# Attention, a low-rank mix, two feed-forward layers and a Fourier mix on one core: tables, decoding, mix and Fourier step placed elsewhere

## The chip, the core and the metric

The kernel runs on one core of a Trainium2 chip. The metric is the device time of one execution in microseconds. The engines are named as in the profile: PE (TensorE, matrix products and transposes), PEld (its weight loads), DVE (VectorE), ACT (ScalarE), POOL (GpSimd) and SP (SyncE, which here only issues transfers). Each engine works through its own instructions in the order in which they stand.

## What is computed

The reference, cut to what matters (x has 2 batches of 768 tokens with 512 columns; attention has 8 heads of width 64):

```
attn: scores = q k^T / 8 - slope_h * dist   (only keys j < n_global, or 0 <= i-j < n_local)
      x      = softmax(scores) v            (heads side by side: 512 columns)
mix:  u = x + (V^T U^T x along the tokens)  (U 768x32, V 32x768)
ffn:  x = u + relu(u @ w1) @ w2             (w1 512x2048, w2 2048x512)
fft:  u = x + real(fft over tokens and columns of x)
      un = (u - mean) / sqrt(var + 1e-6)
ffn:  out = u + relu(un @ w1') @ w2'
```

## The kernel before, in words

Float32 products of full accuracy are made of three matmuls each: every operand is split in a high part (float32r) and a low part (the rest). The weights U, V, w1, w2 arrive as 64-bit doubles. `decode` (L150) turns them into float32 in four operations, on ACT L155 and then on DVE L157, L159 and L161; a decoded chunk of weights (`w_load`, L110, brings it) is written to a scratch in DRAM for the later blocks and split into `wh` (ACT L170) and `wo` (POOL L173, two halves).

The program runs in three stages.

**Attention.** `setup` (L44) loads the first q, k and v, lets POOL write distances into the buffer `vb1` (`rel_make`), and lets DVE make from them two bias tables `dist0` and `dist1` of 1024 columns (`attn_setup`, L391; the second is half the first, ACT L405); a flag `oki` decides a branch. Then `attn` (L452) goes through 24 units (a pair of heads c, a pair of token tiles j and j+3), two units per iteration d = 0 to 11, with three more iterations for the end. An iteration makes scores on PE (L472, L477) in four PSUM banks `acc`, adds the bias and takes the minimum on DVE (L494), exponentials on ACT (L506), transposes on PE (L515), copies them out on DVE (L526) or ACT (L524), multiplies by v one iteration later (L540, two PSUM banks `sd`), and turns the result back two iterations later (L553, DVE L561) into `xall`. Loads of q and k (`qk_load`, L426) and of v (`v_load`, L437) for pair c+2 go out when the buffers of pair c are free. SP issues them in its order.

**Beside the attention** `arm` (L854) steps other generators, one item per step of attention: `lr_setup` decodes U and V, `w_first` decodes the first two chunks of weights, `lr(0)` makes the low-rank sum of batch 0 (L330, L337) and its mix (L346, DVE L347), with transposes of the mixed tiles into `uT` (PE L270, ACT L272, DVE L273) which the first feed-forward step needs. All of these take the two PSUM banks `h`, as the attention's transposes do.

**Feed-forward.** `ffn` (L177) runs 96 steps c, 16 for each of three blocks of four token tiles and each of two layers. A step is 12 matmuls L194 (into `h`), a ReLU split in two (ACT L201, DVE L202) and 12 matmuls L222 (into the four `acc` banks); it yields four times. `drive` (L828) puts side work between yields: after each of n yields a counter grows by a rate, and each whole unit takes one item of a side generator; what is left after n yields is drained at once. Beside block 1 (c = 16 to 31) transposes stand, beside block 2 (c = 32 to 47) the loads of the Fourier tables, a wait until six tiles are done (`lead`), the Fourier step of batch 0 (`fft(0)`: folds on DVE L693 to L711, matmuls L742, L746, L753, L766, L779, L792) and layernorm with transposes of tiles 0 to 3 (`norm`, L811). Layer 1 begins at c = 48 and needs those four. `fft(1)` stands beside c = 48 to 63. A scheduler sets each engine's final order from the program; instructions marked with `keep` stay in program order.

Of the kernel before, what the change touches and what calls it, by code (L numbers as in the profile page):

```python
# [7 lines left out]
F32 = mybir.dt.float32  # L8
# [29 lines left out]
class Prog:  # L38
# [5 lines left out]
    def setup(self, ctx):  # L44
# [13 lines left out]
        nf = cp.tile([P, 2, 2], F32, name="nf")  # L58
        nc.vector.tensor_copy(nf, ni)
        hi = cp.tile([P, 2], F32, name="nhi")  # L60
        nc.vector.scalar_tensor_tensor(hi, nf[:, :, 0], 0.0, nf[:, :, 1], ALU.is_lt, ALU.add)
        nv = cp.tile([P, 4], F32, name="nv")
        nc.vector.scalar_tensor_tensor(nv[:, 0:2], hi, 4294967296.0, nf[:, :, 0], ALU.mult, ALU.add)
        self.ng, self.nl, self.nl4 = nv[:, 0:1], nv[:, 1:2], nv[:, 2:3]
        self.attn_setup()
        nc.vector.tensor_scalar(ok[:, 0:1], nv[0:1, 0:1], float(NG_MAX), None, ALU.is_le)
        nc.vector.tensor_scalar(ok[:, 1:2], nv[0:1, 1:2], 1.0, None, ALU.is_ge)
        nc.vector.scalar_tensor_tensor(ok[:, 0:1], nv[0:1, 1:2], float(NL_MAX), ok[:, 0:1], ALU.is_le, ALU.mult)
        nc.vector.tensor_tensor(ok[:, 0:1], ok[:, 0:1], ok[:, 1:2], ALU.mult)
        oki = cp.tile([1, 1], I32, name="oki")  # L70
        nc.vector.tensor_copy(oki, ok[:, 0:1])
# [192 lines left out]
    def transpose_in(self, layer, i, src):  # L264
# [3 lines left out]
        tp = self.psum("tr")  # L268
# [47 lines left out]
    def w_first(self):  # L316
        for c in range(2):
            for z in range(4):
                self.w_word(c, z)
                yield  # L320
        self.w_split(0)
        yield


    def lr(self, b, pool, tiles):
# [12 lines left out]
        R = pool.tile([P, D], FR, tag="R", bufs=1, name=f"R{b}")  # L338
        nc.scalar.copy(R, rps)
        nc.vector.tensor_tensor(R[64:128, :], rps[64:128, :], R[64:128, :].bitcast(F32), ALU.subtract)  # L340
        yield
        for t in range(NT):
            i = b * NT + t
            x = self.x[i]
            hp = self.psum("m")
# [16 lines left out]
    def rel_make(self):  # L362
# [12 lines left out]

        blocks = ((0, 0, 1), (3, 128, -1), (4, 256, -1), (5, 511, -1), (1, 0, 1), (2, 128, 1), (6, 127, -1), (7, 255, -1))
# [10 lines left out]
        iota(self.key[:, 0:P], 0, 1, 0)  # L387
        iota(self.key[:, P:], 0, 1, 0)

    def attn_setup(self):  # L390
        nc = self.nc  # L391
# [50 lines left out]
    def attn(self, pool):  # L442
# [75 lines left out]
        def turned(d, g):  # L518
# [4 lines left out]
            if g == 1 or (g == 3 and d % 2 == 1):  # L523
# [41 lines left out]
        for d in range(ND2 + 3):  # L565
# [288 lines left out]
def arm(tc, pg, fast):  # L854
    with ExitStack() as ctx1:
# [186 lines left out]
```

## Time and profile before

| quantity | value |
|---|---|
| time, median of 3 runs | 701.17 us (700.15 to 703.96) |
| the profiled execution's own time | 699.38 us |
| its span from first to last instruction | 697.5 us |
| PE busy in the span | 666.3 us (96%) |
| DVE busy | 362.4 us (52%) |
| POOL busy | 311.5 us (45%) |
| ACT busy | 283.2 us (41%) |
| mean granted clock of PE | 0.989 of full |

The profiled execution took 1.88 us more than its span and 1.79 us less than the median. Busy time of an engine is a sum over stages, so it doesn't say by itself which engine ends last in a stage; that is read in the windows, the timelines and the chain of waits.

### The profile page before, as it was taken

The numbers are of one execution on the slowest core, as the hardware profiler recorded it, in microseconds if no ns is written. First come the engines' busy times: TensorE is split into PE (matmuls) and PEld (weight loads), VectorE is DVE, ScalarE is ACT, GpSimd is POOL, SyncE is SP. The second block draws the span as 40 slices with busy tenths as digits, with TensorE's granted clock in tenths as the row PEclk, the third lists the DMA queues.
The fourth block names the chain that finished last, engine by engine and source line by source line (L and its number), as shares of the span: only waits on it lengthen the run. The fifth ranks groups of instructions, "written<-read, shape, count | busy, mean of one in ns | idle before, by whom it ended". The sixth has DMA issues, their size and how long they took to land.

```text
span 697.5 us, 9519 instructions
## 1 busy us (share of the span) xinstructions
PE 666.3 (96%) x3498; PEld 546.7 (78%) x3498; DVE 362.4 (52%) x702; ACT 283.2 (41%) x513; POOL 311.5 (45%) x288
## 2 busy tenths in 40 slices
PE   7998889999999999999999879999999999999996
PEld 6877566887778888887888767888888888888885
DVE  6899677888839453388535878116632111211112
ACT  5898642543434434334433324222323333232330
POOL 4022102554675654557443637344644444544441
PEclk9999999999999999999999989999999999999999
DMA  8967503787897777666744321312142232332301
GB/s 283 326 239 268 182 1 97 220 249 248 251 363 242 250 251 246 233 215 220 268 176 146 133 85 38 114 61 90 61 151 92 93 113 95 132 110 96 115 32 66
DMA packets 34424, 115.98 MB, mean 166 GB/s; under 512 B 4096, under 2 KB 5568, under 8 KB 31296
## 3 DMA queue, kind: packets, MB, share of 16 engines
q1 hardware_dynamic: 32544, 111.04, 47.3%
q0 software_dynamic: 1392, 3.65, 1.6%
q8 instruction: 29, 0.48, 0.3%
q10 hardware_dynamic: 432, 0.59, 0.3%
q14 instruction: 27, 0.22, 0.1%
HBM read 95.34 MB, written 19.92 MB: 165 GB/s over the span
## 4 chain that ended last, share of the span: by engine, by line
PE 73%; DVE 15%; ACT 4%; DMA 3%; issue 2%; POOL 2%; SPq 0%; DVEq 0%; ACTq 0%; POOLq 0%
PE ps_acc L222 32%; PE ps_h L194 31%; DVE wr L159 2%; DVE w L161 2%; DVE p L494 2%; PE ps_sd L540 2%; POOL wo L173 2%; DMA qk<-qkg 1%; PE ps_sd L270 1%; ACT wr L155 1%; PE ps_sd L742 1%; PE ps_sd L766 1%; PE ps_acc L472 1%; DVE pt L526 1%; DVE xall L561 1%
## 5 line engine op out<-in xcount | busy, mean ns | idle before, releaser
L173 POOL TENSOR_TENSOR wo<-w,wh 128x512 fp32r<-128x512 f32 x192 | 270.2, 1428 | 271.0 <-ACT wh L170 270.8
L194 PE MATMUL ps_h<-uT,wh 128*128 128x512 f32 x768 | 238.7, 392 | 1.3 <-ACT uT L272 1.3
L202 DVE SCALAR_TENSOR_TENSOR gl<-ps_h,gh 128x512 fp32r<-128x512 f32 x96 | 66.0, 687 | 234.0 <-ACT gh L201 233.9
L170 ACT CAST wh<-w 128x1024 fp32r<-128x1024 f32 x96 | 101.0, 1052 | 196.7 <-PE ps_acc L222 122.9
L194 PEld LDWEIGHTS ps_h<-uT,wh 128*128 128x128 f32 x768 | 143.2, 188 | 32.5 <-issue 2.2
L222 PE MATMUL ps_acc<-wh,gl 128*128 128x512 f32 x384 | 151.4, 394 | 2.3 <-DVE gl L202 2.1
L222 PE MATMUL ps_acc<-wh,gh 128*128 128x512 f32 x384 | 152.1, 396 | 0.0
L194 PE MATMUL ps_h<-uT,wo 128*128 128x512 f32 x384 | 150.1, 391 | 1.9 <-POOL wo L173 1.9
L222 PE MATMUL ps_acc<-wo,gh 128*128 128x512 f32 x384 | 150.4, 392 | 0.0
L201 ACT ACTIVATE gh<-ps_h 128x512 fp32r<-128x512 f32 x96 | 57.4, 598 | 139.9 <-PE ps_h L194 137.2
L222 PEld LDWEIGHTS ps_acc<-wh,gl 128*128 128x128 f32 x384 | 72.5, 189 | 20.1 <-DVE gl L202 4.8
L194 PEld LDWEIGHTS ps_h<-uT,wo 128*128 128x128 f32 x384 | 72.1, 188 | 18.1 <-POOL wo L173 2.9
L222 PEld LDWEIGHTS ps_acc<-wo,gh 128*128 128x128 f32 x384 | 72.7, 189 | 14.1
L222 PEld LDWEIGHTS ps_acc<-wh,gh 128*128 128x128 f32 x384 | 72.6, 189 | 13.8
L159 DVE SCALAR_TENSOR_TENSOR wr<-wr 128x1024 int32<-128x1024 int32 x32 | 48.2, 1506 | 12.2 <-ACT wr L155 10.9
L506 ACT ACTIVATE p<-p,m 128x256 f32<-128x256 f32 (+2 forms) x96 | 47.6, 498 | 9.7 <-DVE m L494 9.5
L494 DVE CUSTOM_DVE_ANT_0 p<-ps_acc,dist 128x256 f32<-128x256 f32 (+2 forms) x96 | 34.9, 418 | 7.6 <-PE ps_acc L472 4.2
L155 ACT ACTIVATE wr<-wr 128x1024 f32<-128x1024 f32 x32 | 36.7, 1147 | 0.0
L472 PE MATMUL ps_acc<-qk 64*128 64x256 f32 (+1 forms) x192 | 24.6, 381 | 2.9 <-DVE m L494 2.3
L161 DVE SCALAR_TENSOR_TENSOR w<-wr 128x1024 int32<-128x1024 int32 x16 | 26.4, 1652 | 0.8
L515 PE MATMUL ps_h<-ident,p 128*128 128x128 f32 x144 | 22.1, 288 | 2.9 <-DVE xall L561 2.2
L540 PE MATMUL ps_sd<-pt,vb 128*64 128x128 f32 x384 | 23.6, 276 | 0.0
(150 smaller groups left out, 537.5 us busy)
## 6 DMA issues: line engine op xcount, KB each, us to landing
w<-wscr SPq DMA_DIRECT2D x80, 512.0 KB, 3.3
wr<-wl SPq DMA_DIRECT2D x17, 1024.0 KB, 7.5
wr<-wl SPq DMA_DIRECT2D x60, 256.0 KB, 5.5
wscr<-w SPq DMA_DIRECT2D x16, 512.0 KB, 7.7
wscr<-wd SPq DMA_DIRECT2D x16, 512.0 KB, 2.9
qk<-qkg SPq DMA_DIRECT2D x7, 1088.0 KB, 7.1
vb<-vw SPq DMA_DIRECT2D x8, 768.0 KB, 4.7
out<-qk SPq DMA_DIRECT2D x11, 256.0 KB, 3.4
```

The source lines that it names most:

```text
L155: keep(nc.scalar.activation(hi.bitcast(F32), hi.bitcast(F32), AF.Copy, scale=2.0 ** -112))
L159: nc.vector.scalar_tensor_tensor(lo, hi, 3, lo, ALU.logical_shift_left, ALU.bitwise_or)
L161: nc.vector.scalar_tensor_tensor(out.bitcast(I32), hi, -2147483648, lo, ALU.bitwise_and, ALU.bitwise_or)
L170: nc.scalar.copy(hi, raw)
L173: nc.gpsimd.tensor_tensor(lo[:, h], raw[:, h], hi[:, h].bitcast(F32), ALU.subtract)
L194: nc.tensor.matmul(hp, lhsT=w[:, s], rhs=u[:, dd, :], start=n == 0, stop=n == 11)
L201: nc.scalar.activation(gh, hp, AF.Relu)
L202: nc.vector.scalar_tensor_tensor(gl, hp, 0.0, gh.bitcast(F32), ALU.max, ALU.subtract)
L222: nc.tensor.matmul(acc[t], lhsT=g[:, s], rhs=w[:, D:2 * D], start=pf == 0 and m == 0, stop=pf == NF - 1 and m == 2)
L494: keep(nc.vector.tensor_tensor_reduce(out=T[z][:, s], in0=sp[z][:, s], in1=self.dist[z][:, dcol[t]:dcol[t] + width[t]], op0=ALU.add, op1=A ...
L506: keep(nc.scalar.activation(T[z][:, s], T[z][:, s], AF.Exp, bias=m[:, z, y:y + 1], scale=-1.0, accum_out=sm[:, u % 2, y, z:z + 1]))
L540: keep(nc.tensor.matmul(pv[z * HD:(z + 1) * HD, g:g + P], lhsT=v[:, vc, z * HD:(z + 1) * HD], rhs=pt[z][:, o:o + P], start=i == 0, stop=i ...
```

## The change

It has four parts.

1. `setup`: the integers n are used directly (the cast into `nf` goes), the flag takes three operations and not five, and `attn_setup` is split. Part 0 makes the columns that the first unit needs (0 to 128, 384 to 768) ahead of the branch, part 1 the other columns (128 to 384, 768 to 1024) after the first unit's L494. All of it stays in program order.
2. `turned`: in the last iteration (d = 11) all copies go to ACT.
3. `arm`: the items are in another order. The decoding of U comes later, that of the first weights one operation per iteration half, that of V behind it, that of the second weights behind the low-rank sum. `lr` is cut in `lr_sum` and `lr_mix`; the mix of batch 0 and its transposes take banks `acc`, at the end of attention.
4. The Fourier tables are loaded beside block 1, so that `fft(0)` and `norm` are the only side work of block 2, at a rate of 0.55.

```diff
-        nc.vector.tensor_copy(nf, ni)
-        nc.vector.scalar_tensor_tensor(hi, nf[:, :, 0], 0.0, nf[:, :, 1], ALU.is_lt, ALU.add)
+        nc.vector.scalar_tensor_tensor(hi, ni[:, :, 0], 0.0, ni[:, :, 1], ALU.is_lt, ALU.add)
...
-        self.attn_setup()
...
+        self.attn_setup(0)
...
+        iota(self.key[:, 0:P], 0, 1, 0)
+        iota(self.key[:, P:], 0, 1, 0)
         blocks = ((0, 0, 1), (3, 128, -1), (4, 256, -1), (5, 511, -1), (1, 0, 1), (2, 128, 1), (6, 127, -1), (7, 255, -1))
...
-        for c0, c1, blocks in ((0, 128, ((0, P),)), (384, 768, ((512, 32),)), (128, 384, ((256, 32),)),
-                               (768, WTAB, ((896, 32),))):
+        for c0, c1, blocks in (((0, 128, ((0, P),)), (384, 768, ((512, 32),))),
+                               ((128, 384, ((256, 32),)), (768, WTAB, ((896, 32),))))[part]:
...
-            if g == 1 or (g == 3 and d % 2 == 1):
+            if g == 1 or (g == 3 and d % 2 == 1) or d == ND2 - 1:
...
                 for y in range(2):
                     soft(u0, y)
                     exps(u0, y)
+                if d == 0:
+                    self.attn_setup(1)
                 soft(u1, 0)
...
-                for _ in pg.lr_setup(lp):
-                    step(att, 1)
+                step(att, 3)
                 pg.w_load(1)
-                step(att, 2)
+                low = pg.lr_setup(lp)
+                for _ in range(2):
+                    next(low)
+                    step(att, 2)
+                for _ in pg.w_first(0):
+                    step(att, 2)
                 pg.w_load(2)
-                for _ in pg.w_first():
+                for _ in low:
                     step(att, 1)
                 while pg.heads < 8:
                     step(att, 1)
-                for _ in pg.lr(0, lp, range(0, 4)):
+                step(att, 1)
+                for _ in chain(pg.lr_sum(0, lp), pg.w_first(1)):
                     step(att, 1)
                 while not pg.att_tail:
                     step(att, 1)
+                pg.w_split(0)
+                mix = pg.lr_mix(0, range(0, 4), "sc")
+                for _ in range(4):
+                    step(mix, 2)
+                    step(att, 1)
+                drain(mix)
...
-        drive(main, 64, pg.tr_gen(0, range(8, 12), pg.x), 0.3)
...
-        drive(main, 64, chain(pg.fft_tables(), lead(pg, 6), pg.fft(0), pg.norm(range(0, 4))), 0.5)
+        drive(main, 64, chain(pg.tr_gen(0, range(8, 12), pg.x), pg.fft_tables()), 0.3)
+        drive(main, 64, chain(lead(pg, 6), pg.fft(0), pg.norm(range(0, 4))), 0.55)
```

Where instructions come to stand, as the two built programs have them (line numbers of the changed kernel are three lower in the attention and the feed-forward part):

DVE at the start, the kernel before: the tables (`dist_66` is dist0, `vb_69` is vb1) ahead of the first unit's reads (`L494`).

```order
L71 CAST oki<-ok 1x1
L400 TENSOR_SCALAR dist_66<-vb_69,nv 128x128
L401 TENSOR_TENSOR dist_66<-dist_66,vb_69 128x128
L400 TENSOR_SCALAR dist_66<-vb_69,nv 128x384
L401 TENSOR_TENSOR dist_66<-dist_66,vb_69 128x384
L400 TENSOR_SCALAR dist_66<-vb_69,nv 128x256
L396 TENSOR_SCALAR vb_69<-vb_69,nv 128x160
L401 TENSOR_TENSOR dist_66<-dist_66,vb_69 128x256
L404 SCALAR_TENSOR_TENSOR dist_66<-vb_69,nv,dist_66 128x128
L404 SCALAR_TENSOR_TENSOR dist_66<-vb_69,nv,dist_66 128x32 x2
L400 TENSOR_SCALAR dist_66<-vb_69,nv 128x256
L401 TENSOR_TENSOR dist_66<-dist_66,vb_69 128x256
```

DVE at the same place, the changed kernel, from the last table operation ahead of the branch to the second unit.

```order
L401 SCALAR_TENSOR_TENSOR dist_66<-vb_69,nv,dist_66 128x32
L936 TENSOR_LOAD oki
L937 COMPARE_AND_BRANCH
L491 ISA p_208,m_210<-ps_acc,dist_66 128x128
L491 ISA m_210 128x1
L491 ISA p_209,m_210<-ps_acc,dist_67 128x128
L491 ISA m_210 128x1
L491 ISA p_208,m_210<-ps_acc,dist_66 128x384
L491 ISA m_210 128x1
L491 ISA p_209,m_210<-ps_acc,dist_67 128x384
L491 ISA m_210 128x1
L397 TENSOR_SCALAR dist_66<-vb_69,nv 128x256
```

The last two of the four column ranges (six operations, of which the last row shows the first) moved from ahead of the first unit to behind it.

DVE at the end of attention, the kernel before, from the copy behind the last L494 (`uT_1298` is the low part for the first feed-forward block, `xall_200` batch 0, `xall_201` batch 1).

```order
L526 COPY pt_1273<-ps_sd 128x512
L347 TENSOR_TENSOR xall_200<-ps_h,xall_200 128x512
L699 MEMSET vb_68 128x1
L273 TENSOR_TENSOR uT_1298<-ps_h,uT_1297 128x4x128
L549 TENSOR_SCALAR sm_922<-sm_922 128x8
L550 RECIPROCAL sm_922<-sm_922 128x8
L561 TENSOR_TENSOR xall_201<-ps_h,sm_922 128x2x128 x2
L526 COPY pt_1320<-ps_h 128x512
L347 TENSOR_TENSOR xall_200<-ps_h,xall_200 128x512
L526 COPY pt_1340<-ps_h 128x512
L526 COPY pt_1344<-ps_sd 128x512
L273 TENSOR_TENSOR uT_1298<-ps_h,uT_1297 128x4x128
```

The same place in the changed kernel (`uT_1385` is the low part, `xall_188` batch 0, `wr_589` the second weights).

```order
L334 TENSOR_TENSOR R_1271<-ps_h,R_1271 64x512
L546 TENSOR_SCALAR sm_904<-sm_904 128x8
L547 RECIPROCAL sm_904<-sm_904 128x8
L558 TENSOR_TENSOR xall_189<-ps_h,sm_904 128x2x128 x2
L523 COPY pt_1288<-ps_h 128x512
L154 TENSOR_SCALAR wr_589<-wr_589 128x1024
L344 TENSOR_TENSOR xall_188<-ps_acc,xall_188 128x512
L156 SCALAR_TENSOR_TENSOR wr_589<-wr_589 128x1024
L546 TENSOR_SCALAR sm_1004<-sm_1004 128x8
L344 TENSOR_TENSOR xall_188<-ps_acc,xall_188 128x512
L547 RECIPROCAL sm_1004<-sm_1004 128x8
L158 SCALAR_TENSOR_TENSOR w_1290<-wr_589 128x1024
```

The mix reads `ps_acc` where it read `ps_h`, the decoding of the second weights moved in between, and the copies of the last iteration are gone from DVE.

PE where layer 0 ends (c = 48), the kernel before: the last Fourier matmuls and the four transposes for layer 1.

```order
L779 MATMUL ps_sd<-c_2870,fpt_3302 128x258
L781 MATMUL ps_sd<-sgn,fpr_3303 128x258
L270 MATMUL ps_sd<-ident,vb_68 128x128 x4
L222 MATMUL ps_acc<-wh_3625,gh_3706 128x512
L222 MATMUL ps_acc<-wo_3626,gh_3706 128x512
L222 MATMUL ps_acc<-wh_3625,gl_3707 128x512
L270 MATMUL ps_sd<-ident,vb_68 128x128 x4
L222 MATMUL ps_acc<-wh_3625,gh_3706 128x512
```

In the changed kernel the first of these four transposes stands five steps sooner, ahead of the matmuls of a later step.

```order
L219 MATMUL ps_acc<-wh_3364,gh_3458 128x512
L219 MATMUL ps_acc<-wo_3365,gh_3458 128x512
L219 MATMUL ps_acc<-wh_3364,gl_3459 128x512
L267 MATMUL ps_sd<-ident,vb_68 128x128 x4
L191 MATMUL ps_h<-uT_2217,wh_3501 128x512
```

The four transposes stand at c = 43, 44, 45 and 46; the first Fourier matmuls (`L741`, L742 of before), which stood at c = 41, stand at c = 35 and 36, and `L745` (L746 of before), which needs `em`, at c = 36.

## Rows read from the trace of the kernel before

**Rows 1.** The page, part 1: busy time, share of the span and instructions.

```profile
PE 666.3 (96%) x3498; PEld 546.7 (78%) x3498; DVE 362.4 (52%) x702; ACT 283.2 (41%) x513; POOL 311.5 (45%) x288
```

**Rows 2.** Windows, us: length; busy (count) PE, PEld, DVE, ACT, POOL; PEclk; DMA; GB/s.

```profile
60.00:80.00 20.00, 16.66 (x157) 11.79 (x158) 15.32 (x54) 15.21 (x43) 5.85 (x5) 0.91 0.74 254
400.00:420.00 20.00, 15.27 (x60) 11.67 (x61) 14.25 (x29) 4.49 (x7) 7.33 (x12) 0.83 0.26 80
```

**Rows 3.** The chain that ended last, 0 to 130 us: start, length, what.

```profile
12.98 10.08 DMA qk<-qkg
23.24 0.84 POOL qk L430
```

**Rows 4.** Timeline of DVE at the start: start, length, operation, count, idle before.

```profile
8.55 0.34 DVE L400 TENSOR_SCALAR dist<-vb,nv 128x256 f32<-128x256 f32 x1
...
9.39 0.25 DVE L404 SCALAR_TENSOR_TENSOR dist<-vb,nv,dist 128x32 f32<-128x32 f32 x1
10.24 0.29 DVE L494 CUSTOM_DVE_ANT_0 p<-ps_acc,dist 128x128 f32<-128x128 f32 x1 [0.60 <-DVE dist L404]
...
11.62 0.42 DVE L494 CUSTOM_DVE_ANT_0 p<-ps_acc,dist 128x256 f32<-128x256 f32 x1
```

**Rows 5.** Timeline of PE in attention, same columns.

```profile
24.12 0.93 PE L472 MATMUL ps_acc<-qk 64*128 64x128 f32 x8 [0.55 <-POOL qk L430]
...
30.45 1.79 PE L472 MATMUL ps_acc<-qk 64*128 64x256 f32 x16
...
74.37 3.60 PE L330 MATMUL ps_h<-xall,ur 128*32 128x512 f32 x12 [2.42 <-DVE xall L561]
...
86.41 2.00 PE L472 MATMUL ps_acc<-qk 64*128 64x256 f32 x16
...
111.03 0.73 PE L194 MATMUL ps_h<-uT,wh 128*128 128x512 f32 x2
```

**Rows 6.** Timeline of DVE in attention, two stretches, same columns.

```profile
55.66 0.69 DVE L157 TENSOR_SCALAR wr<-wr 128x1024 int32<-128x1024 int32 x1
56.45 1.23 DVE L159 SCALAR_TENSOR_TENSOR wr<-wr 128x1024 int32<-128x1024 int32 x1
...
58.30 1.21 DVE L161 SCALAR_TENSOR_TENSOR w<-wr 128x1024 int32<-128x1024 int32 x1
...
90.61 0.42 DVE L494 CUSTOM_DVE_ANT_0 p<-ps_acc,dist 128x256 f32<-128x256 f32 x1
...
107.49 0.69 DVE L273 TENSOR_TENSOR uT<-ps_h,uT 128x512 fp32r<-128x512 f32 x1 [2.17 <-ACT uT L272]
...
108.60 0.76 DVE L561 TENSOR_TENSOR xall<-ps_h,sm 128x256 f32<-128x256 f32 x2
```

**Rows 7.** Timeline of PE, c = 36 and c = 47 to 48.

```profile
318.77 0.50 PE L194 MATMUL ps_h<-uT,wo 128*128 128x512 f32 x1 [1.49 <-POOL wo L173]
...
403.21 1.09 PE L270 MATMUL ps_sd<-ident,vb 128*128 128x128 f32 x4 [3.45 <-DVE mv L818]
...
410.74 1.23 PE L194 MATMUL ps_h<-uT,wh 128*128 128x512 f32 x3 [1.30 <-ACT uT L272]
```

**Rows 8.** One window of 1 us, columns as in rows 2.

```profile
404.00:405.00 1.00, 1.00 (x5) 0.80 (x4) 0.77 (x2) 0.59 (x1) 0.58 (x2) 0.50 0.25 98
```

**Rows 9.** Timeline of DVE in the folds of fft(0).

```profile
302.06 2.04 DVE L159 SCALAR_TENSOR_TENSOR wr<-wr 128x1024 int32<-128x1024 int32 x1
...
318.92 1.51 DVE L693 TENSOR_TENSOR qk<-dist 128x255 f32<-128x255 f32 x1
...
321.21 0.42 DVE L704 TENSOR_TENSOR em<-qk,em 1x258 fp32r<-1x258 f32 x1
```

**Rows 10.** Timeline of POOL, the split of weights.

```profile
301.72 3.52 POOL L173 TENSOR_TENSOR wo<-w,wh 128x512 fp32r<-128x512 f32 x2 [2.91 <-ACT wh L170]
```

**Rows 11.** Timeline of PE, where steps 41 and 42 begin.

```profile
347.48 0.63 PE L194 MATMUL ps_h<-uT,wh 128*128 128x512 f32 x2
...
354.76 0.63 PE L194 MATMUL ps_h<-uT,wh 128*128 128x512 f32 x2
```

More of the change, by code (lines that the diff above doesn't have):

```diff
@@ L262, in uT_tiles, with transpose_in @@
         return self.uT[key]
-    def transpose_in(self, layer, i, src):
+    def transpose_in(self, layer, i, src, kind="tr"):
         nc = self.nc
@@ L267, in transpose_in @@
         s = slice((i % 4) * P, (i % 4 + 1) * P)
-        tp = self.psum("tr")
+        tp = self.psum(kind)
         for dd in range(ND):
@@ L314, in lr_setup, with w_first, lr_sum @@
         yield
[L316 to L325, printed above, removed]
+    def w_first(self, c):
+        for z in range(4):
+            self.w_word(c, z)
+            yield
+    def lr_sum(self, b, pool):
         nc = self.nc
@@ L337, in lr @@
         nc.tensor.matmul(rps, lhsT=self.band.rearrange("p z r -> p (z r)"), rhs=part, start=True, stop=True)
-        R = pool.tile([P, D], FR, tag="R", bufs=1, name=f"R{b}")
+        self.R = R = pool.tile([P, D], FR, tag="R", bufs=1, name=f"R{b}")
         nc.scalar.copy(R, rps)
@@ L341, in lr, with lr_mix @@
         yield
+    def lr_mix(self, b, tiles, kind="m"):
+        nc, R = self.nc, self.R
         for t in range(NT):
@@ L344, in lr @@
             x = self.x[i]
-            hp = self.psum("m")
+            hp = self.psum(kind)
             nc.tensor.matmul(hp, lhsT=self.vs[:, t * P:(t + 1) * P], rhs=R, start=True, stop=True)
@@ L349, in lr @@
             if t > 0 and i - 1 in tiles:
-                self.transpose_in(0, i - 1, self.x[i - 1])
+                self.transpose_in(0, i - 1, self.x[i - 1], kind)
                 yield
         if b * NT + NT - 1 in tiles:
-            self.transpose_in(0, b * NT + NT - 1, self.x[b * NT + NT - 1])
+            self.transpose_in(0, b * NT + NT - 1, self.x[b * NT + NT - 1], kind)
             yield
@@ L386, in rel_make, with attn_setup @@
                 nc.gpsimd.memset(rel[0:1, 3 * P:5 * P], float(-4 * FAR))
[L387 to L391, printed above, removed]
+    def attn_setup(self, part):
+        nc, keep = self.nc, self.tc.keep_in_program_order
         rel, key = self.rel, self.key
@@ L891, in arm @@
                 drain(pg.lr_setup(lp))
-                drain(pg.w_first())
+                for c in range(2):
+                    drain(pg.w_first(c))
+                pg.w_split(0)
                 pg.attn_any(pool)
-                drain(pg.lr(0, lp, range(0, 4)))
+                drain(chain(pg.lr_sum(0, lp), pg.lr_mix(0, range(0, 4))))
         pg.side_mode = True
-        drive(main, 64 - ahead, chain(pg.lr(1, lp, range(6, 8)), pg.tr_gen(0, range(4, 6), pg.x)), 0.45)
-        drive(main, 64, pg.tr_gen(0, range(8, 12), pg.x), 0.3)
+        drive(main, 64 - ahead, chain(pg.lr_sum(1, lp), lambda: pg.lr_mix(1, range(6, 8)),
+                                      pg.tr_gen(0, range(4, 6), pg.x)), 0.45)
     with ExitStack() as ctx3:
         pg.fft_open(ctx3)
-        drive(main, 64, chain(pg.fft_tables(), lead(pg, 6), pg.fft(0), pg.norm(range(0, 4))), 0.5)
+        drive(main, 64, chain(pg.tr_gen(0, range(8, 12), pg.x), pg.fft_tables()), 0.3)
+        drive(main, 64, chain(lead(pg, 6), pg.fft(0), pg.norm(range(0, 4))), 0.55)
         drive(main, 64, chain(pg.norm(range(4, 6)), lead(pg, 12), pg.fft(1), pg.norm(range(6, 8))), 0.5)
```

24 lines of the change are left out of this document (11 added, 13 removed).

## The prediction, made before the changed kernel ran

> **What bounds the kernel now.** I began with busy time: PE works 666.3 of 697.5 us [rows 1], so at most some 31 us of the span can go without removing matmuls, and the change removes none. The next view is windows of 20 us, to see where those 31 us lie. Most windows after 200 us are full; the gaps are in attention (60 to 80 us: PE 16.66 of 20 at a granted clock of 0.91) and where layer 0 ends (400 to 420 us: 15.27 at 0.83) [rows 2]. The change touches these two places and leaves the feed-forward steps as they are. The chain of waits says what ends last at the start: the load of q and k for the third head pair, 12.98 to 23.06 us, and its scaling on POOL [rows 3]. The timelines of PE and DVE then give each term.
>
> **Part 1, the tables.** Three operations on one range of 256 columns take from 8.55 to 9.64 us [rows 4]; two such ranges, some 2 us, leave the path to the first unit, and the cast with them, so the first L494 starts at about 8.3 instead of 10.24. But part 1 then stands ahead of the second unit's L494, which started at 11.62 [rows 4]: 8.3, plus the first unit's 1.4 us (10.24 to 11.62), plus 2 us is 11.7. So only the first unit is sooner. What decides the third iteration is the load in [rows 3]. In the changed SP order the load of v for pair 1 waits for part 1 (it overwrites the table's source) and the q and k load stands behind it, with one V (a copy of 192 KB) more ahead than before; two copies behind each other landed 0.9 us apart. I take +0.9 us, with bounds −0.3 (transfers that had waited for the tables go sooner) and +1.0. ACT, POOL and the flag are hidden behind that load, so the removed small operations give nothing: without that cover they would be worth the 1.9 us above.
>
> **Part 3, the middle.** Iteration d = 3 starts at 24.12 and d = 4 at 30.45: 6.33 us, which PE fills [rows 5]. From 24.12 to 86.41 (d = 11) are eight intervals, 62.29 us, where eight times 6.33 is 50.6: 11.7 us extra. They are the decoding that stands in one piece on DVE (for one chunk of weights 0.69 + 1.23 + 1.21 = 3.1 us [rows 6]; V has three quarters of the columns, about 2.4), twice for weights, and the sum L330, for which PE waits 2.42 us and then works 3.60 at the reduced clock [rows 5]; behind it comes the wait for R. In the changed order the second chunk's decoding is gone from here, the first is spread over four places, and L330 stands an iteration later, when batch 0 is long complete. DVE has per iteration eight L494 at 0.345 apart, two or three copies at 0.6 and 1.2 us for L561 and its helpers, 5.2 to 5.8 us, so it can take 0.5 to 1.1 us of decoding for nothing. What is left of the 11.7: 1.0 for V (it stands in one piece, less the spare time), 1.2 for the first weights (between 0.5 and 2.1), 0.5 for U, which used to lie in the wait of [rows 3] and no longer does, and 1.9 for L330 at the full clock (half of 3.60, and a little). That is 4.6, so d = 11 starts at 24.12 + 0.9 + 50.6 + 4.6 = 80.2; with some friction I take 80.8, 5.6 us sooner (bounds 3 and 8).
>
> **Parts 2 and 3, the tail.** From 86.41 to the first L194 at 111.03 are 24.6 us [rows 5]. The last L494 is issued 4.2 us after the start and done at 4.9 (90.61 of [rows 6] and the next two entries' time); then DVE must do its tail. In the trace it idles there between small chained operations, up to 2.17 us for ACT's copy [rows 6], because mix, transposes and the attention's own transposes share two banks. In the changed order DVE has 2 copies, R, three times L561 with helpers (108.10 to 109.27, 1.17 us; [rows 6] has its start of 108.60), the second decoding 2.9, five mixes at 0.62 and four L273 at 0.62 until the uT of tile 3 is there: 1.2 + 0.6 + 3.5 + 2.9 + 3.1 + 2.5 + 0.4 = 14.2. That is a floor of 4.9 + 14.2 = 19.1. The old tail had 6.9 us of idle DVE in nine pieces, the largest of them the 2.17 above; with four `acc` banks I grant half, 3.2. So 22.3, a gain of 2.3 (bounds 0 and 4.5). The moved decoding is hidden if DVE would have idled there, else it costs its 2.9. The copies that go to ACT cost nothing there: ACT is the engine waiting for PE and DVE in this stage. SP's third weight load now goes ahead of q and k for pair 4; that is 2 us of transfer ahead of a buffer that was 5 us early.
>
> Attention together: 5.6 + 2.3 = 7.9 us, range 3 to 11.
>
> **Part 4, the Fourier step.** In the kernel before 40 items wait for 32 places, so the rest is drained at c = 48: four layernorm transposes follow each other with nothing between. PE waits 3.45 us for the statistics and 1.30 for uT [rows 7], and after the first of these it runs at half its clock [rows 8]. Against the full pitch I count, from 397 to 421 us, 0.8 + 3.6 + 2.2 (the clock) + 1.5 + 0.9 = 9.0 us. In the changed order the first Fourier matmul stands five and a half steps sooner, and the transposes stand at c = 43 to 46 with whole steps between; these 9.0 go. What is late next is the front: `em` is ready on DVE at about 321.6 (L704 at 321.21 [rows 9]), late because folds, weight decoding and the ReLU's L202 share DVE. PE would want it at about 316.8. In the changed order L704 stands ahead of one L202 and comes at 319.4 to 320.3, so PE waits 2.5 to 3.4 us where it stood 1.49 for `wo` [rows 7] (1.65 with what follows). An idle of this length was followed by the half clock at [rows 5] and [rows 8], so I add 1.7 for it. New wait 2.9 + 1.7 − 1.65 = 2.95; the boundary gives 9.0 − 2.95 = 6.1, I take 6.3 as the clock may hold. Bounds 3 and 8.6.
>
> A rule bears on that front. First the row: L159 takes 1.23 us by itself [rows 6] and 2.04 where POOL's split of weights runs [rows 9, 10]; L693 between POOL's operations takes 1.51, three times the similar ones around it. The Trainium skill ("SBUF — State Buffer", Who interferes with whom) says that a DVE instruction with two SBUF inputs and a GpSimd instruction that reads SBUF exclude each other for the whole instruction. The trace agrees in kind. What it would do here is rival B.
>
> **The sum.** 699.38 − 7.9 − 6.3 = 685.2 for the profiled execution. The median stands 1.79 above it, so 687.0.
>
> **The rivals.** B, the front eats the boundary: each of the six two-input operations ahead of L704 waits for a POOL split, which from [rows 9] is 0.8 to 1.1 us each, so `em` is 4 to 5 us later than I put it, and only some 1.5 us of the 6.3 are left: 691.8. For it: the folds in [rows 9]. Against: POOL is not always reading then, and those rows have their share of it already. C, the tail does not pay: the chain PE to DVE to ACT at the end is one of dependences, four more banks don't shorten it, and the second decoding costs its 2.9 there; attention gives 3, so 691.9. For it: the idle times there end on ACT's copies [rows 6], not on banks. D, more: no wait at the front and the tail near its floor: 1.79 + 699.38 − 11 − 8.6 = 681.6. E, the change does not do what it says: the scheduler had loaded the tables at about 200 us anyway, and the transposes at c = 43 to 46 wait as they did at 48, while the tail only swaps its waits: 698 to 703. F, slower: the sixteen groups of Fourier matmuls of block 2 now come a step and a half behind their operands instead of six, and PE goes in order, so each may wait for a copy or a subtraction that DVE does behind decoding. The gain of 14.2 is gone at 0.9 us per group; at 1.1 it is 704.6. Against it: steps 41 to 42 hold the same groups beside the same decoding and take 7.28 us [rows 11], which is 5.44 for the step and 1.8 for the Fourier matmuls, without a wait.
>
> **How the numbers follow.** Forecast A, 683.0 to 690.5: 0.57. B 0.15, C 0.13, D 0.07, E 0.04, F 0.04. From the bounds, 11 + 8.6 and 3 + 3, the forecast's ends would be 681.6 and 695.2; B and C lie inside, D at the lower end. The range is 681 to 695, which leaves out E, F and a part of D, C and B beyond. A measurement of this kernel tells about 0.5%, 3.5 us, from no change. Faster by more (below 697.7): A, B, C, D and a little of the rest, 0.91. Within: 0.05. Slower: 0.04.
>
> **What would show it right or wrong.** In the changed kernel's trace: the first L491 at 8.3 and the second unit's at 11.7; d = 3 at 25.0; d = 11 at 80.8; the first L191 at 103.1; one wait of PE of 2.5 to 3.4 us at `L745` near c = 36, the clock below full behind it; no gap over 0.5 us at c = 48. It is wrong if the tail stays at 24 us or more (C), if PE waits at several groups between c = 35 and 42 (B, F), or if the transposes of layernorm still meet a wait for statistics (E).

## The result, and the profile after

The changed kernel takes 683.09 us (median of 4, 681.38 to 685.25), the kernel before beside it 700.66 (median of 4, 697.94 to 703.96): ratio 0.9749, 95% interval 0.9698 to 0.98. The profiled execution took 681.38 us with a span of 679.6, where before it was 699.38 and 697.5. That is 17.9 us less of span, against 14.2 forecast for the profiled execution; the median of 683.1 lies 3.9 under the 687.0 forecast and inside the range.

The page of the changed kernel, part 1 (columns as in rows 1), shows PE 6.7 us less busy for the same 3498 matmuls, at a mean granted clock of 0.995 where it was 0.989. The other 11.2 us of the 17.9 are idle time of PE that went.

```profile
PE 659.6 (97%) x3498; PEld 545.8 (80%) x3498; DVE 362.1 (53%) x697; ACT 285.4 (42%) x515; POOL 310.0 (46%) x288
```

The windows of 20 us (columns as in rows 2) at the places that were short before, and at the front of the Fourier step:

```profile
60.00:80.00 20.00, 17.48 (x199) 13.96 (x197) 16.89 (x66) 17.08 (x58) 5.72 (x5) 1.00 0.57 198
300.00:320.00 20.00, 16.91 (x72) 14.17 (x71) 14.21 (x29) 8.25 (x14) 9.07 (x11) 0.91 0.65 213
380.00:400.00 20.00, 20.00 (x94) 16.57 (x92) 10.37 (x15) 8.11 (x10) 9.92 (x8) 1.00 0.48 178
400.00:420.00 20.00, 20.00 (x91) 16.55 (x91) 16.66 (x33) 8.36 (x16) 14.21 (x16) 1.00 0.22 79
```

The stretch from 380 us, in which layer 0 now ends (c = 48 at 392.8), is full at the full clock; in [rows 2] the stretch in which it ended had 15.27 of 20 at 0.83. A new shortage stands at 300 to 320. Attention went from 16.66 to 17.48 in the window from 60 us and no longer falls in clock there.

PE's timeline in attention (rows as in [rows 5]; L469 is the scores, L191 the first feed-forward matmul, L324 the low-rank sum):

```profile
13.26 1.94 PE L469 MATMUL ps_acc<-qk 64*128 64x128 f32 x8 [1.91 <-POOL band L297]
...
24.01 0.93 PE L469 MATMUL ps_acc<-qk 64*128 64x128 f32 x8
...
55.61 2.00 PE L469 MATMUL ps_acc<-qk 64*128 64x256 f32 x16
58.70 1.17 PE L512 MATMUL ps_h<-ident,p 128*128 128x128 f32 x8 [1.09 <-DVE xall L558]
...
63.15 0.93 PE L469 MATMUL ps_acc<-qk 64*128 64x128 f32 x8
...
78.55 1.91 PE L324 MATMUL ps_h<-xall,ur 128*32 128x512 f32 x12 [1.90 <-ACT pt L521]
80.39 2.00 PE L469 MATMUL ps_acc<-qk 64*128 64x256 f32 x16
...
101.83 0.40 PE L191 MATMUL ps_h<-uT,wh 128*128 128x512 f32 x1
102.93 0.50 PE L191 MATMUL ps_h<-uT,wh 128*128 128x512 f32 x1 [0.70 <-DVE uT L270]
```

With the starts of feed-forward steps read from the same view, the 17.9 us are found like this (the difference is what the changed kernel is ahead at that point):

| point | before, us | after, us | ahead | gained since the point above |
|---|---|---|---|---|
| d = 3, first scores | 24.12 | 24.01 | 0.11 | 0.11 |
| d = 11, first scores | 86.41 | 80.39 | 6.02 | 5.91 |
| c = 8 | 158.52 | 150.17 | 8.35 | 2.33 |
| c = 35 | 311.22 | 301.48 | 9.74 | 1.39 |
| c = 50 | 421.00 | 404.52 | 16.48 | 6.74 |
| c = 95 | 683.39 | 665.95 | 17.44 | 0.96 |
| end of the span | 697.5 | 679.6 | 17.9 | 0.46 |

I take c = 8 and not the first L191 as the end of the tail, since the first L191 at 101.83 is followed by a wait of 0.70 for uT, so 0.85 of the 9.20 us by which it comes sooner are given back in the first steps.

### The profile page after: what moved, and what is told of

The parts are those of the page before. It is cut to its first block, busy times and chain, and to the rows that moved or that the text cites. A ratio compares the mean times of both kernels' runs of the same rounds, so it can differ in the third digit from the quotient of the medians.

```text
span 679.6 us, 9505 instructions
## 1 busy us (share of the span) xinstructions
PE 659.6 (97%) x3498; PEld 545.8 (80%) x3498; DVE 362.1 (53%) x697; ACT 285.4 (42%) x515; POOL 310.0 (46%) x288
## 4 chain that ended last, share of the span: by engine, by line
PE 66%; DVE 7%; ACT 2%; issue 1%; POOL 1%; DMA 1%; SPq 0%; DVEq 0%; ACTq 0%; POOLq 0%
PE ps_acc L219 31%; PE ps_h L191 30%; DVE w L158 2%; DVE wr L156 2%; ACT wr L152 1%; PE ps_sd L267 1%; PE ps_sd L765 1%; PE ps_sd L778 1%; POOL wo L170 1%; ACT wh L167 1%; PE ps_sd L741 1%; DMA wr<-wl 1%; PE ps_sd L791 1%; DVE qk L692 0%; DVE gl L199 0%
## 5 line engine op out<-in xcount | busy, mean ns | idle before, releaser
L191 PE MATMUL ps_h<-uT,wh 128*128 128x512 f32 x768 | 238.3, 391 | 0.7 <-DVE uT L270 0.7
L199 DVE SCALAR_TENSOR_TENSOR gl<-ps_h,gh 128x512 fp32r<-128x512 f32 x96 | 65.9, 686 | 231.6 <-ACT gh L198 231.5
L191 PEld LDWEIGHTS ps_h<-uT,wh 128*128 128x128 f32 x768 | 143.3, 188 | 30.7 <-DVE uT L270 1.1
L191 PE MATMUL ps_h<-uT,wo 128*128 128x512 f32 x384 | 149.7, 390 | 0.0
L191 PEld LDWEIGHTS ps_h<-uT,wo 128*128 128x128 f32 x384 | 72.2, 188 | 15.4
L491 DVE CUSTOM_DVE_ANT_0 p<-ps_acc,dist 128x256 f32<-128x256 f32 (+2 forms) x96 | 35.0, 418 | 7.2 <-PE ps_acc L469 4.0
L427 POOL TENSOR_SCALAR qk<-qk 128x768 f32<-128x768 f32 x6 | 5.0, 834 | 50.0 <-DMA qk<-qkg 27.1
L469 PE MATMUL ps_acc<-qk 64*128 64x256 f32 (+1 forms) x192 | 24.7, 380 | 2.3 <-POOL band L297 1.9
```

Of the source, the lines that this page charges most:

```text
L191: nc.tensor.matmul(hp, lhsT=w[:, s], rhs=u[:, dd, :], start=n == 0, stop=n == 11)
L199: nc.vector.scalar_tensor_tensor(gl, hp, 0.0, gh.bitcast(F32), ALU.max, ALU.subtract)
L469: keep(nc.tensor.matmul(sp[z][:, o:o + n], lhsT=q[r, t * P:(t + 1) * P], rhs=win(k[r], t), start=True, stop=True))
L491: keep(nc.vector.tensor_tensor_reduce(out=T[z][:, s], in0=sp[z][:, s], in1=self.dist[z][:, dcol[t]:dcol[t] + width[t]], op0=ALU.add, op1=A ...
```

## The experiments

Two stretches serve as yardsticks: from d = 11 to c = 8 (the tail), and from c = 35 to c = 50 (the Fourier step, the end of layer 0 and the two transposes behind it). Iteration d = 3 starts between 23.6 and 25.8 us from run to run, and how long PE runs at the half clock behind its wait at 13 us goes with that: with d = 3 at 24.01, in the changed kernel, the granted clock was 0.50 from 14 to 16 us, with d = 3 at 25.79, in the kernel with the copies back, from 14 to 20 us. So phases are compared from d = 3 on. The second yardstick has a scatter of the same kind: seven kernels of the table have the changed kernel's Fourier part, and their stretch from c = 35 takes 103.04 to 105.00 us. In the longest (tables whole) PE waits 3.09 us for `em` as in the changed kernel, but the half clock behind it lasts some 6 us instead of 3. One window of 1 us, 4 to 5 us behind the wait, first in that kernel and then in the changed one:

```profile
314.00:315.00 1.00, 1.00 (x4) 0.71 (x4) 0.00 (x0) 0.15 (x1) 0.77 (x1) 0.50 1.01 322
```

```profile
314.00:315.00 1.00, 1.00 (x6) 0.83 (x5) 0.00 (x0) 0.72 (x1) 0.20 (x1) 1.00 0.88 256
```

Each ratio in the table is to runs of the kernel before that were made beside that kernel; their medians lie between 698.65 and 700.66 us.

| kernel | time, us | ratio to before (95%) | d = 3 to 11 | d = 11 to c = 8 | c = 35 to 50 |
|---|---|---|---|---|---|
| before | 700.66 | 1 | 62.29 | 72.11 | 109.78 |
| changed | 683.09 | 0.9749 (0.9698 to 0.98) | 56.38 | 69.78 | 103.04 |
| Fourier part undone | 688.70 | 0.9863 (0.9824 to 0.9902) | 56.50 | 69.82 | 109.52 |
| Fourier part alone | 694.29 | 0.9926 (0.9893 to 0.996) | 62.13 | 72.13 | 103.17 |
| mix in banks h | 688.62 | 0.9863 (0.9826 to 0.99) | 56.41 | 75.84 | 103.07 |
| tables whole | 682.36 | 0.9742 (0.9715 to 0.9768) | 56.26 | 69.63 | 105.00 |
| copies back | 683.36 | 0.9759 (0.9735 to 0.9784) | 56.39 | 70.22 | 103.41 |
| second decoding with V | 686.06 | 0.9794 (0.9765 to 0.9823) | 59.05 | 70.07 | 104.47 |
| two idle items | 679.45 | 0.9723 (0.9689 to 0.9757) | 56.34 | 69.80 | 100.36 |
| folds cut | 680.01 | 0.9716 (0.9691 to 0.9741) | 56.31 | 69.80 | 100.50 |
| changed, again | 683.73 | 0.9794 (0.9762 to 0.9826) | 56.35 | 69.80 | 103.35 |
| sum in sd, two idle items | 677.71 | 0.9695 (0.9666 to 0.9723) | 54.50 | 71.28 | 100.61 |
| split on DVE | 678.53 | 0.9706 (0.967 to 0.9742) | 56.31 | 69.78 | 100.22 |
| all three | 677.96 | 0.9704 (0.9684 to 0.9723) | 54.27 | 69.79 | 100.33 |

**Do the parts add up?** The Fourier part was undone in the changed kernel, and set alone in the kernel before.

```diff
-        drive(main, 64, chain(pg.tr_gen(0, range(8, 12), pg.x), pg.fft_tables()), 0.3)
-        drive(main, 64, chain(lead(pg, 6), pg.fft(0), pg.norm(range(0, 4))), 0.55)
+        drive(main, 64, pg.tr_gen(0, range(8, 12), pg.x), 0.3)
+        drive(main, 64, chain(pg.fft_tables(), lead(pg, 6), pg.fft(0), pg.norm(range(0, 4))), 0.5)
```

> The changed kernel with its fourth part alone undone: the Fourier tables stand beside block 2 again, at the rate of 0.5. Theory (the parts lie behind each other on PE and add up): attention as in the changed kernel, first L191 near 101.8 us; the idle of PE behind c = 47 is back, the wait of 3.1 us near c = 36 is gone; the span grows by what c = 35 to 50 gave in the changed kernel, 16.48 - 9.74 = 6.7 us, so about 689.8 us against 683.1. Rival (the later start of block 2 in the kernel before made the layer's end late, so the gain belongs to attention): less than 3 us longer, below 686.

> The kernel before with the fourth part alone. Theory (parts add up): first L194 near 111.0 as before, c = 48 some 8 us sooner, the time 6.7 us below the kernel before, near 694; a wait of about 3 us on em near c = 36 and the lower clock behind it, as in the changed kernel. Rival: with attention as it was, the loads and the decoding stand otherwise at c = 36, and the wait on em is absent or twice as long: 690 or 697.

Undone, the waits of [rows 7] are back, almost to the hundredth (PE, the transposes for layer 1 and its first matmul):

```profile
393.00 1.08 PE L267 MATMUL ps_sd<-ident,vb 128*128 128x128 f32 x4 [3.44 <-DVE mv L817]
...
400.53 1.23 PE L191 MATMUL ps_h<-uT,wh 128*128 128x512 f32 x3 [1.27 <-ACT uT L269]
```

Alone, the wait on `em` is there as in the changed kernel, though attention is the old one:

```profile
319.63 0.69 PE L746 MATMUL ps_sd<-alt,em 128*128 128x386 f32 x1 [3.07 <-DVE em L704]
```

The stretch from c = 35 takes 109.5 and 103.2 us, the values of before and changed. So the fourth part is worth 6.5 us with the new attention and 6.6 with the old, and the parts add up: 5.3 us of median alone and 5.6 less when undone, within their intervals. The rivals, that this gain belongs to attention or that the wait differs, fell.

**What shortens the tail?** First, the mixes were put back into the two shared banks.

```diff
-                mix = pg.lr_mix(0, range(0, 4), "sc")
+                mix = pg.lr_mix(0, range(0, 4))
```

> The changed kernel, where the mix of batch 0 and its transposes take the two banks h again, in the same place of the program. Theory (the free acc banks shorten the tail): from the scores of d = 11 to the first L191 23.5 us instead of 21.4, the time near 685.2. Rival (the tail is shorter since mix and decoding stand behind the last scores, whatever the bank): within 0.5 us of the changed kernel, 683.

PE of this kernel, the scores of d = 11 and the first L191:

```profile
79.97 2.00 PE L469 MATMUL ps_acc<-qk 64*128 64x256 f32 x16
...
109.24 0.73 PE L191 MATMUL ps_h<-uT,wh 128*128 128x512 f32 x2
```

29.3 us instead of 21.4, and 75.8 us to c = 8 instead of 69.8: 6.1 us longer, where I had expected 2. It is also 3.7 longer than in the kernel before, so in the tail the new order would have been a loss without the new banks. The rows show how: a mix L344 waits for its matmul, and the next transposes on PE wait until L344 has read its bank `h`. (Part of the 6.1 us is clock: it is at 0.50 from 102 to 104 us in this kernel.)

```profile
104.66 0.69 DVE L344 TENSOR_TENSOR xall<-ps_h,xall 128x512 f32<-128x512 f32 x1 [2.26 <-PE ps_h L343]
```

```profile
105.49 0.63 PE L550 MATMUL ps_h<-ident,xT 128*128 128x128 f32 x4 [0.88 <-DVE xall L344]
```

In the changed kernel one such wait of a mix is left, since the third mix has a bank of its own but follows the transposes in PE's order:

```profile
97.39 0.69 DVE L344 TENSOR_TENSOR xall<-ps_acc,xall 128x512 f32<-128x512 f32 x1 [1.95 <-PE ps_acc L343]
```

Next, the copies of the last iteration were put back from ACT to DVE.

> The changed kernel with the last iteration's copies on DVE and ACT as before. Theory (DVE waits 1.95 us for the mix matmul in the tail, so two copies of 0.6 us fit): first L191 within 0.5 us of 101.8, the time within 0.7 us. Rival (DVE sets the tail): both copies are paid, 1.2 us longer.

```diff
-            if g == 1 or (g == 3 and d % 2 == 1) or d == ND2 - 1:
+            if g == 1 or (g == 3 and d % 2 == 1):
```

```profile
25.79 0.93 PE L469 MATMUL ps_acc<-qk 64*128 64x128 f32 x8
...
82.18 2.00 PE L469 MATMUL ps_acc<-qk 64*128 64x256 f32 x16
...
104.41 0.50 PE L191 MATMUL ps_h<-uT,wh 128*128 128x512 f32 x1 [0.44 <-ACT uT L269]
```

From d = 11 the first L191 takes 22.2 us instead of 21.4, 0.8 longer, between the theory's 0.5 and the rival's 1.2. By c = 8 it is 70.22 us instead of 69.78, 0.4 longer, and the time doesn't tell it from the changed kernel. The span was 3.1 us longer, but 1.8 of that is the start (d = 3 at 25.79), which the edit doesn't touch. So by c = 8 the theory is the nearer: two copies of 0.6 us find most of their room in DVE's waits.

Then the second decoding was put back into the middle, each operation ahead of the like one of V.

```diff
-                for _ in low:
-                    step(att, 1)
+                second = pg.w_first(1)
+                for _ in low:
+                    next(second, None)
+                    step(att, 1)
...
-                for _ in chain(pg.lr_sum(0, lp), pg.w_first(1)):
+                for _ in pg.lr_sum(0, lp):
```

> The changed kernel with the decoding of the second weights in the middle, one operation beside each of V's, and not in the tail. Theory (in the tail the 3 us of DVE work lie partly in idle time): d = 11 some 2.5 to 3 us later than 80.4, the tail 1 to 1.5 us shorter than 21.4, the time 1 to 2 us longer, near 684.5. Rival (DVE is the tail's limit, so the decoding costs the same in either place): d = 11 later by 3, the tail shorter by 3, no difference.

PE of this kernel (d = 3, the transposes of d = 10, d = 11, the first L191):

```profile
25.00 0.93 PE L469 MATMUL ps_acc<-qk 64*128 64x128 f32 x8
...
75.58 1.16 PE L512 MATMUL ps_h<-ident,p 128*128 128x128 f32 x8 [2.48 <-DVE xall L558]
...
84.05 2.00 PE L469 MATMUL ps_acc<-qk 64*128 64x256 f32 x16
...
103.34 0.49 PE L191 MATMUL ps_h<-uT,wh 128*128 128x512 f32 x1
```

In the middle PE waits 2.48 us for DVE where it waited 0.6, and d = 3 to 11 takes 59.05 us, 2.7 more. The first L191 follows d = 11 by 19.3 us instead of 21.4, which looks like the rival's even trade, but by c = 8 it is 70.07 against 69.78: the 2.1 us are given back within the first steps. So the decoding costs 2.7 us in the middle and nothing that lasts in the tail. My theory had the sign; the size was 3.0 where I had expected 1 to 2.

**Is the table split worth anything?** Here both parts of the tables are made ahead of the loop.

```diff
         self.attn_setup(0)
+        self.attn_setup(1)
...
-                if d == 0:
-                    self.attn_setup(1)
```

> The changed kernel with both parts of the tables ahead of the branch again (the small operations on the flag stay as changed). Theory (the first unit is not on the path, since PE next waits for the second pair's q and k, landed at 12.0 us): first L491 at 10.2 instead of 8.6 us, d = 3 within 0.5 us of 24.0, the time within 1 us of the changed kernel (683). Rival (the split is worth what it takes from the path to the first unit): d = 3 at 25.6, 1.6 us longer.

```profile
11.66 3.37 PE L470 MATMUL ps_acc<-qk 64*128 64x256 f32 x15 [3.03 <-DVE m L492]
...
23.60 0.93 PE L470 MATMUL ps_acc<-qk 64*128 64x128 f32 x8
```

Iteration d = 3 starts at 23.60 us, none later than the 24.01 with the split, and the time is 0.7 us lower, inside the intervals. The split gives nothing at d = 3: the rival fell. The theory's reason is not what the first row shows, though: PE waits there for DVE's reads of the first unit (L492, the L491 of the changed kernel), not for the second pair's q and k.

**What is the new wait made of?** Two idle items behind the folds put the first Fourier matmuls a step later.

```diff
         fold(P, xm, False, em, None, 0)
         yield
+        for _ in range(2 if b == 0 else 0):
+            yield
```

> The changed kernel with two items that do nothing behind the folds of fft(0), so that its first matmuls come one step later and em at c = 37.0 instead of 36.0. Theory (the new wait of 3.1 us and the half clock behind it are only the front of fft(0) coming too early): both go, 3.1 + 1.4 = 4.5 us less, near 678.6, and the transposes for layer 1 still end before c = 48. Rival (DVE is late for every group of fft(0), not just for em): the wait moves to a later group or to the layernorm transposes, less than 1.5 us gained, 681.6 or more.

The wait on `em` and the half clock behind it go, yet of 4.5 us only 2.7 are gained, and a wait on `gl` stands at c = 36:

```profile
312.99 0.50 PE L219 MATMUL ps_acc<-wh,gl 128*128 128x512 f32 x1 [0.94 <-DVE vb L698]
```

Cutting the folds in smaller items lets L199 (the `gl` of that step) go first.

```diff
             fold(P, E, False, ee[0][:, i, :], ee[1][:, i, :], i)
+            if b == 0 and i > 0:
+                yield
```

> The changed kernel with the folds of tiles 1 and 2 of fft(0) cut in two items, which gives the same places on PE as the two idle items did, and lets the ReLU's L199 go ahead of folds on DVE. Theory (what was left of the front's cost with the idle items is L199 and the split of weights standing behind folds on DVE): the wait of 1.1 us on gl at c = 36 goes, c = 35 to 48 takes 1 us less than the 88.6 there, the time about 678.5. Rival (PE waits for any of DVE's work there, its order doesn't matter): 679.5 or more, with the wait in another place.

The wait on `gl` went, and one on `wo` of 1.5 us came, of the size of that in [rows 7]; the stretch is as long as with the idle items (100.50 and 100.36). The rival stands here: the wait moves.

```profile
309.79 0.50 PE L191 MATMUL ps_h<-uT,wo 128*128 128x512 f32 x1 [1.51 <-POOL wo L170]
```

What makes DVE late there? Its folds beside POOL's split, in the changed kernel: DVE, and below it POOL.

```profile
306.12 1.53 DVE L692 TENSOR_TENSOR qk<-dist 128x255 f32<-128x255 f32 x1
307.57 1.22 DVE L693 COPY qk<-dist 128x2 f32<-128x2 f32 x1
```

```profile
306.08 2.69 POOL L170 TENSOR_TENSOR wo<-w,wh 128x512 fp32r<-128x512 f32 x2 [0.43 <-ACT wh L167]
```

POOL's row is two subtractions, of which the first ends at 307.37. The copy of two columns ends as the second does (306.08 + 2.69 = 308.77, 307.57 + 1.22 = 308.79), and the fold on `dist` ends 0.28 us behind the first. So in one run the split of these two chunks was put on DVE, behind `em`.

```diff
-            nc.gpsimd.tensor_tensor(lo[:, h], raw[:, h], hi[:, h].bitcast(F32), ALU.subtract)
+            eng = nc.vector if c in (36, 37) else nc.gpsimd
+            eng.tensor_tensor(lo[:, h], raw[:, h], hi[:, h].bitcast(F32), ALU.subtract)
```

> The changed kernel with the split of two chunks of weights (c = 36 and 37) on DVE and not on POOL; on DVE it stands behind em. Theory (the folds ahead of em are slow since POOL reads SBUF at the same time): the fold L692 on dist takes 0.41 us and not 1.53, the copy of two columns 0.15 and not 1.22, the wait on em falls from 3.1 to about 0.9 us; 1 us or so is given back for wo on DVE. Rival (their slowness is from where their data lie, not from POOL): 1.5 and 1.2 us as before, the wait stays at 3 us.

The same DVE operations, and PE's wait on `em`:

```profile
306.15 0.41 DVE L693 TENSOR_TENSOR qk<-dist 128x255 f32<-128x255 f32 x1
306.48 0.16 DVE L694 COPY qk<-dist 128x2 f32<-128x2 f32 x1
```

```profile
308.27 0.44 PE L746 MATMUL ps_sd<-alt,em 128*128 128x386 f32 x1 [0.91 <-DVE em L704]
```

0.41 and 0.16 us instead of 1.53 and 1.22, and 0.91 us of wait instead of 3.09, without the half clock behind it. This is what the theory said. The time is 678.53 us, 5.2 under the changed kernel beside it; the stretch from c = 35 gives 2.8 to 3.1 of that in the profiles. The two profiled executions, 681.86 and 678.65 us, differ by no more than that; the rest lies inside the spread of the changed kernel's runs (681.86 to 686.89). It was not given back for `wo`.

**Can both kernels be beaten by more?** The last three edits were measured beside the changed kernel, run once more.

> The changed kernel once more, unchanged, to stand beside the other runs of this call on one chip. Every theory expects 683 us, 0.975 of the kernel before, with d = 3 at 24 us, give or take 1.8 us for the first loads.

It took 683.73 us, 0.9794 of the kernel before, which agrees with the first measurement within the intervals: the change is worth 2.1 to 2.5%. The low-rank sum's wait at 78.55 us is for ACT's copy that frees its bank:

```diff
     def lr_sum(self, b, pool):
         nc = self.nc
-        tps = self.psum("m")
+        tps = self.psum("pv")
```

In this run the two idle items of above stood too.

> The changed kernel with the two idle items ahead of the matmuls of fft(0), and the low-rank sum L324 in a bank sd and not h. Theory (L324 waits 1.90 us for ACT's copy only because that copy frees its bank h, while a bank sd is free 2 us sooner): the wait goes, the interval from d = 10 to d = 11 takes 9.0 us instead of 10.9, and with the 1.5 to 2.7 us of the idle items the time is near 679.5, 3.5 to 4 below the changed kernel. Rival (ACT and the copies set that iteration, the bank is chance): d = 11 not sooner, the time that of the idle items alone, some 681.

PE of this kernel (d = 11, the transposes behind it, the first L191), and a window of 2 us in it:

```profile
79.05 2.00 PE L469 MATMUL ps_acc<-qk 64*128 64x256 f32 x16
...
88.80 1.84 PE L512 MATMUL ps_h<-ident,p 128*128 128x128 f32 x8 [0.62 <-DVE xall L558]
...
101.98 0.39 PE L191 MATMUL ps_h<-uT,wh 128*128 128x512 f32 x1
```

```profile
90.00:92.00 2.00, 2.00 (x13) 1.67 (x14) 2.00 (x4) 1.47 (x3) 0.00 (x0) 0.50 0.00 0
```

The wait went, d = 3 to 11 takes 54.50 us instead of 56.35, as expected. But from d = 11 to the first L191 are 22.9 us instead of 21.4: a granted clock of 0.50 there goes with the loss of most of it (this execution, 679.59 us, was the slowest of six, of which the fastest took 676.51). The last run has the same bank and the same short waits, and its clock stayed up:

```profile
90.00:92.00 2.00, 2.00 (x33) 1.83 (x33) 2.00 (x4) 1.26 (x3) 0.00 (x0) 1.00 0.00 0
```

That run joins this bank, the split on DVE and one idle item behind the folds:

```diff
         yield
+        if b == 0:
+            yield
```

> What the runs so far point to, in one kernel: the changed kernel with the split of c = 36 and 37 on DVE, one idle item ahead of the matmuls of fft(0), and the low-rank sum in a bank sd. Theory (the wait on em was two things, POOL's reads and the early place): the 0.91 us that were left of it go, and the sum's bank gives the 0.4 us to the first L191 that were left of its 1.9; 1.3 us less than with the split alone, near 677. Rival (with DVE's order changed, wo or gl is late again, as with the idle items): no better than the split alone, 678.5.

In it d = 3 to 11 takes 54.27 and d = 11 to the first L191 again 21.4 us, so the sum's bank is worth 2 us in the profile in which the clock held (by the medians, the two kernels with it stay within the interval of the split alone). From c = 35 on it is no better than the split alone (100.33 and 100.22): `em` is waited for no longer, but `wo` is, once late on DVE and once on POOL:

```profile
307.74 0.50 PE L192 MATMUL ps_h<-uT,wo 128*128 128x512 f32 x1 [0.53 <-DVE wo L171]
...
365.96 0.50 PE L192 MATMUL ps_h<-uT,wo 128*128 128x512 f32 x1 [1.20 <-POOL wo L171]
```

So the rival held for that half. Three kernels, at 677.7, 678.0 and 678.5 us, are the fastest here, 0.970 of the kernel before, and their intervals don't tell them apart. The stretch from c = 35 stayed at 100.2 to 100.6 us in each of the five kernels with an edit at the front; what holds it there was not tried.

## Why the prediction was right, step by step

- **Tables.** The first L491 was forecast at 8.3 and the second unit's at 11.7; DVE shows 8.63 and 12.04. That the second unit gains nothing held, and the run with whole tables, where its first L492 stands at 11.90, confirms it.

```profile
8.63 0.29 DVE L491 CUSTOM_DVE_ANT_0 p<-ps_acc,dist 128x128 f32<-128x128 f32 x1 [0.60 <-PE ps_acc L474]
...
12.04 0.42 DVE L491 CUSTOM_DVE_ANT_0 p<-ps_acc,dist 128x256 f32<-128x256 f32 x1
```

- **The load for the third pair** was the step that failed. I put +0.9 us on it, for one V more ahead of it on SP, with −0.3 as the lower bound, and took it for what decides d = 3. It came sooner, not later, and it no longer decides. The scaling behind that load starts at 21.38, where it was 23.24 [rows 3], and is done at 22.21, 1.8 us ahead of the scores of d = 3:

```profile
21.38 0.83 POOL L427 TENSOR_SCALAR qk<-qk 128x768 f32<-128x768 f32 x1 [6.90 <-PE ps_sd L512]
```

What sets d = 3 now is PE's own work: it waits 1.91 us ahead of 13.26, and from there to 24.01 its timeline has no wait. The row at 13.26 names POOL's `band`, but that makes nothing for the scores, and POOL's scaling of the second pair's q was done at 12.91. In the changed kernel's second run the same wait ends on DVE's reads of the second unit, which free a bank and stand behind part 1 of the tables:

```profile
13.48 1.95 PE L469 MATMUL ps_acc<-qk 64*128 64x128 f32 x8 [1.91 <-DVE m L491]
```

Kernels with the same start put d = 3 anywhere from 23.6 to 25.8 us, so the 25.0 of the forecast lies inside that scatter, but not for the reason that I gave. Why the load landed sooner stays open. In the changed kernel U and three V were issued from 6.76 to 8.49 us, ahead of the v load that waits for the tables; before, U and two V stood behind it. But the run with whole tables has the old order on SP and issues the q and k load at 14.21, later than before (12.98), and its scaling starts soonest of the three:

```profile
10.00 0.33 SPq L435 DMA_DIRECT2D vb<-vw  x1
10.44 0.37 SPq L281 DMA_DIRECT2D lrt<-U  x1
...
14.21 0.35 SPq L424 DMA_DIRECT2D qk<-qkg  x1
```

```profile
20.47 0.83 POOL L428 TENSOR_SCALAR qk<-qk 128x768 f32<-128x768 f32 x1 [6.09 <-PE ps_h L513]
```

So the order of the issues is not shown to be the reason.
- **The middle.** d = 11 was forecast at 80.8 and came at 80.39. That is luck in part, two misses against each other: d = 3 was 1.0 sooner, and from there it took 56.38 us against 55.8. The parts: the first weights cost 1.2 as forecast (d = 8 takes 55.61 to 63.15, 1.21 over the pitch), V 0.6 (1.0 forecast), U nothing (0.5 forecast), L324 itself 1.9 as forecast. A wait of 1.90 for a bank ahead of L324 was not in the sum, save as 0.6 of friction.
- **The tail** was forecast to give 2.3 up to the first L191. There it gave 3.2 (21.4 us), and 2.33 by c = 8. Rival C fell. That the size came out is in part luck: I had put half of DVE's idle time on the banks (half of 6.9 is 3.45, not the 3.2 of the sum), and they were worth 6.1 us in the new order. In one thing C was right: without the banks the tail would have been longer than before.
- **The boundary** was forecast to give 6.3 and gave 6.74. The 9.0 us at c = 48 went: PE is full at the full clock from 380 to 420 us, and from c = 35 to 50 its timeline names no wait but the one on `em`. The new wait on `em` was forecast at 2.5 to 3.4 us, followed by the half clock; it is 3.09, and a window of 1 us behind it shows the clock at 0.50:

```profile
310.43 0.60 PE L745 MATMUL ps_sd<-alt,em 128*128 128x386 f32 x1 [3.09 <-DVE em L703]
```

```profile
311.00:312.00 1.00, 1.00 (x4) 0.81 (x3) 1.00 (x4) 0.48 (x1) 0.90 (x2) 0.50 0.23 90
```

  Rival B, the front eating the gain, was right about the mechanism (POOL's reads), but its price was in my sum already, since I took the durations from rows that had it.
- **Not forecast** were 1.39 us between c = 8 and c = 35, 0.96 between c = 50 and 95 and 0.46 at the end. In the first, PE waited 0.92 us on `gl` at c = 10 in the kernel before and not in the changed one; that wait is there with the Fourier part alone (0.89) and not with it undone, so it went with the new attention. The second holds a wait of 0.36 on `wo`, which is there with the Fourier part undone and not with it alone. No run tested why either went. With the load (1.0, less the 0.6 of the middle) and the boundary (0.4) they make most of the 3.7 us by which the span fell further than forecast.

## What to carry to other kernels

Ask of a late load what the engine behind it would do without it: before, the load for the third pair ended a wait of only 0.55 us [rows 5], and when it came 1.9 us sooner, an earlier wait and the work behind it set the same start. Where side work moves to a stage that already shares few banks, move its banks with it. And when work is started sooner, look on the engines for what now runs beside it: here DVE's and POOL's reads met, and moving the split of two chunks off POOL gave as much (2.8 us) as starting later (2.7).

## What the runs showed of the hardware that I had not expected

Two DVE operations on SBUF that ran beside POOL's split took 1.53 us (a fold of 255 columns) and 1.22 us (a copy of two columns, which ended with POOL's operation), against 0.41 and 0.16 with the same inputs in the same order when POOL did nothing there. For the copy that is more than sevenfold. The Trainium skill ("SBUF — State Buffer", Who interferes with whom) states of a DVE instruction with two SBUF inputs and a GpSimd instruction that reads SBUF that one blocks the other for the whole instruction; the fold, which has two inputs, agrees with it in these numbers.

Two kernels with the same waits on PE (1.15 us, then 0.62) got different clocks behind them, 0.50 and 1.00 in the window from 90 us, so a wait of this length cost 1.5 us in one and nothing in the other. And the same wait of 3.09 us on `em` was followed by some 3 us at the half clock in one kernel and 6 in another.
